# A decode kernel: four-column-tile PV, looped batches, long runs of w3 and w4, and extra matmuls between the last stages

## The chip, the core and the metric

The kernel runs on one core of one Trainium2 chip. The metric is device time in microseconds (us) of one execution; lower is better. Before the change it takes 193.37 us (median of 4 executions).

Each product is a pair of instructions: a weight load (the stationary operand, "PEld" in the profile) and a matmul (which streams the moving operand, "PE"); the page counts 2,028 of each. DVE, ACT and POOL are the vector, scalar and general engines. SP issues the large DMA transfers.

## The reference, cut to what matters

```python
# A: attention of one new token per sequence; B = 8, D = 512, 32 query heads, 8 KV heads, window 2048
q = (layernorm(x) @ wq)                  # wq [512, 4096]
p = softmax(q k^T / sqrt(128))           # k, v: the last 2048 rows of each cache, 8 x 8 x 2048 x 128
h = x + concat_heads(p v) @ wo           # wo [4096, 512]
# B: mixer and MLP. With sequence length 1 the token shift gives zeros: x1 = layernorm(h)
xb = layernorm(h)
h2 = gelu(layernorm(xb) @ w3) @ w4       # w3 [512, 1792], w4 [1792, 512]
out = h + xb + h2
```

K and V are 67 MB, wq and wo 8.4 MB, w3 and w4 3.7 MB: 79.18 MB in all, read once. Everything else is small.

## The kernel before

Per batch, TensorE transposes K (128 small transposes), multiplies by q, and later by V. The last stages, with h kept transposed: `hT` has the 512 features on 4 x 128 partitions.

```python
# loads at the end of the queue: wo (4 parts), w3 (2 halves), w4 (3 parts)
B_w3.rearrange("(k p) f -> p k f", k=KC)[:, k0:k1, :]        # runs of 3,584 B
B_w4.rearrange("(c p j) n -> p c (j n)", p=128, j=2)         # runs of 2,048 B
...
def pe_PV(...):    # per (batch, head group): 16 matmuls of 512 columns, two column tiles of 64
    ins = e.matmul(pv_ps[gq][64*a:64*(a+1), :]..., pT_sb[:, gq, cc, :], vq[:, cc, :, :], ...)
...
def pe_proj(e):    # 32 x 4 pairs: weights are columns of wo, next to each other (step 1)
    for h in range(NJ):
        for k in range(KC):
            ins = e.matmul(hT_ps[:, k*B:(k+1)*B], wo_at(h)[:, k*128:(k+1)*128], opl[:, h, :], ...)
...                # DVE and ACT: statistics, norms, uT
def pe_h3(e):      # 56 pairs: weights are every second column of w3 (step 2)
    w3_sb[:, kc, c*256:(c+1)*256].rearrange("p (q j) -> p j q", j=2)[:, j, :]
...                # gelu on ACT
def pe_fin(e):     # 14 x 4 matmuls of 128 columns, waits for each part of w4
```

The step of h3's weights follows from w4's layout: if a partition holds j consecutive rows of w4, the gelu output must have its rows in that order, so h3 has to pick every j-th column of w3. In the same way, w3's layout fixes the order of `hT`'s features, and with it the step of the columns of wo in the projection.

## Time and profile before

| | before |
|---|---|
| time, us (4 executions) | 193.37 (193.22 to 193.54) |
| DMA | 79.18 MB, engines 99-100% busy from the second slice to the last but one |
| last part of w4 releases its matmuls at | 188.68 us of a span of 191.5 |
| projection / h3 on TensorE | 3.57 / 1.66 us |

From the page of the profile: busy time and share of the span of each engine, and three rows over 40 equal slices (granted TensorE clock in tenths, DMA busy in tenths, GB/s).

```profile
PE 145.9 (76%) x2028; PEld 99.3 (52%) x2028; DVE 105.2 (55%) x287; ACT 90.3 (47%) x113; POOL 1.9 (1%) x14
PEclk9999999999699999999999999999999999999555
DMA  6999999999999999999999999999999999999991
GB/s 221 438 431 428 428 421 431 433 431 424 431 428 428 435 431 438 431 428 431 426 428 438 431 435 430 428 431 428 428 438 431 431 431 431 431 431 401 418 398 54
```

The DMA row says what bounds the kernel: no slice below 9 until the data are through. The last three clock digits are 5: TensorE runs the last stages at half clock.

The chain of work that ended last, in order of time (start us, us, what):

```profile
166.46 21.54 DMA slots<-in_B_w_dram
188.00 0.04 issue
188.04 0.60 PE b L887 x16
188.64 0.03 issue
188.68 0.41 PE b L887 x8
```

It goes from the w4 load straight into the last matmuls. And the timeline of TensorE's tail (start us, us, line, operands, count, idle time before and its releaser):

```profile
178.06 3.57 PE L796 MATMUL S_ps<-opl,slots 128*128 128x8 bf16 x128
184.34 1.66 PE L857 MATMUL misc<-uT,slots 128*128 128x8 bf16 x56 [1.52 <-DVE uT L833]
186.82 1.02 PE L887 MATMUL b<-slots,gT 128*8 128x128 bf16 x32 [0.51 <-DMA slots<-in_B_w_dram]
188.04 1.02 PE L887 MATMUL b<-slots,gT 128*8 128x128 bf16 x24 [0.20 <-DMA slots<-in_B_w_dram]
```

L796 is the projection, L857 is h3, L887 the last stage. The last stage waited for DMA twice, but only 0.51 and 0.20 us: TensorE arrives shortly before its data.

### The profile page before, as it was taken

The page shows a single profiled execution, that of the slowest core. Times are in us where ns is not written, and L with a number is a line of the kernel's source. Part 1 is how long each engine was busy: PE and PEld are TensorE (multiplying, and loading weights), DVE is VectorE, ACT ScalarE, POOL GpSimd, SP SyncE. Part 2 cuts the span into 40 slices and gives each one's busy share as a digit, 9 for nine tenths or more (in the row PEclk, how much of TensorE's full clock was granted, in tenths as well). Part 3 has the DMA queues.
Part 4 walks back from the last instruction along what each step waited for, and adds up shares of the span by engine and source line. Part 5 has one row for each costly group of instructions (what it writes and reads, how often), then busy time and mean ns, then how long its engine had stood idle before and what let it go on. Part 6 is the DMA issues. An engine that isn't in the chain of part 4 may idle for free. (4 is left out here: it accounts for less than half of the span.)

```text
span 191.5 us, 4850 instructions
## 1 busy us (share of the span) xinstructions
PE 145.9 (76%) x2028; PEld 99.3 (52%) x2028; DVE 105.2 (55%) x287; ACT 90.3 (47%) x113; POOL 1.9 (1%) x14
## 2 busy tenths in 40 slices
PE   2027998796899869886989688968896888776854
PEld 0003876582857455645564547553655465343842
DVE  6401757464268474747474747565665657585141
ACT  3301676862656265536643564447344835406041
POOL 4000000000000000000000000000000000000000
PEclk9999999999699999999999999999999999999555
DMA  6999999999999999999999999999999999999991
GB/s 221 438 431 428 428 421 431 433 431 424 431 428 428 435 431 438 431 428 431 426 428 438 431 435 430 428 431 428 428 438 431 431 431 431 431 431 401 418 398 54
DMA packets 6857, 79.31 MB, mean 414 GB/s; under 512 B 688, under 2 KB 704, under 8 KB 2368
## 3 DMA queue, kind: packets, MB, share of 16 engines
q1 hardware_dynamic: 6832, 79.18, 97.5%
q8 instruction: 6, 0.10, 0.2%
q14 instruction: 3, 0.02, 0.0%
q10 hardware_dynamic: 16, 0.01, 0.0%
HBM read 79.18 MB, written 0.01 MB: 414 GB/s over the span
## 5 line engine op out<-in xcount | busy, mean ns | idle before, releaser
L496 ACT ACTIVATE kT_sb<-kT_ps 128x1024 bf16<-128x1024 bf16 x64 | 64.6, 1028 | 67.3 <-PE kT_ps L473 66.9
L473 PE MATMUL kT_ps<-perm_b,slots 128*128 128x128 bf16 x1024 | 68.5, 223 | 22.9 <-PEq L454 22.8
L473 PEld LDWEIGHTS kT_ps<-perm_b,slots 128*128 128x128 bf16 x1024 | 60.8, 100 | 33.7 <-issue 33.7
L500 DVE COPY kT_sb<-kT_ps 128x1024 bf16<-128x1024 bf16 x64 | 43.3, 688 | 27.1 <-PE kT_ps L473 27.1
L516 PE MATMUL S_ps<-kT_sb,qcur 128*32 128x512 bf16 x256 | 22.5, 387 | 0.8 <-PEq L454 0.8
L546 ACT ACTIVATE P_sb<-S_ps,mtile 128x1024 bf16<-128x1024 f32 x16 | 17.8, 1115 | 2.6 <-DVE mtile L537 2.5
L595 PE MATMUL b<-slots,pT_sb 128*64 128x512 bf16 x128 | 16.5, 384 | 1.2 <-PEq L454 1.2
L577 DVE TENSOR_TENSOR pT_sb<-kT_ps,maskT 128x1024 bf16<-128x1024 bf16 x16 | 10.5, 685 | 10.7 <-PE kT_ps L489 10.7
L595 PE MATMUL misc<-slots,pT_sb 128*64 128x512 bf16 x128 | 15.3, 382 | 0.6 <-PEq L454 0.6
L526 DVE TENSOR_REDUCE mtile<-S_ps 128x1 f32<-128x512 f32 x8 | 5.5, 692 | 13.6 <-PE S_ps L516 13.6
L595 PEld LDWEIGHTS misc<-slots,pT_sb 128*64 128x64 bf16 x128 | 6.8, 109 | 8.4 <-issue 3.6
L595 PEld LDWEIGHTS b<-slots,pT_sb 128*64 128x64 bf16 x128 | 6.2, 109 | 9.2 <-issue 5.7
L516 PEld LDWEIGHTS S_ps<-kT_sb,qcur 128*32 128x32 bf16 x256 | 5.3, 93 | 8.3 <-issue 4.2
L489 PEld LDWEIGHTS kT_ps<-ident_b,P_sb 128*128 128x128 bf16 x128 | 7.2, 98 | 4.1 <-issue 4.1
L489 PE MATMUL kT_ps<-ident_b,P_sb 128*128 128x128 bf16 x128 | 8.7, 219 | 0.6 <-PEq L454 0.6
L611 DVE SCALAR_TENSOR_TENSOR o_sum<-b,mrl,o_sum 128x128 f32<-128x128 f32 x24 | 8.4, 351 | 0.8
L611 DVE SCALAR_TENSOR_TENSOR o_sum<-misc,mrl,o_sum 128x128 f32<-128x128 f32 x24 | 8.4, 351 | 0.8
L395 PE MATMUL S_ps<-slots,xlnT 128*8 128x512 bf16 x32 | 3.6, 626 | 5.7 <-DMA slots<-in_A_wq_dram 5.7
L412 DVE TENSOR_SCALAR q_sb<-S_ps 128x512 bf16<-128x512 f32 x1 | 0.7, 692 | 9.1 <-PE S_ps L395 9.1
L626 DVE CAST o_all<-misc 16x128 bf16<-16x128 f32 x7 | 2.0, 279 | 6.4 <-PE misc L620 6.3
L395 PEld LDWEIGHTS S_ps<-slots,xlnT 128*8 128x8 bf16 x32 | 1.0, 117 | 7.4 <-issue 7.4
L657 ACT ACTIVATE opl<-kT_ps 128x224 bf16<-128x224 f32 x1 | 1.2, 1182 | 6.6 <-PE kT_ps L649 6.6
(104 smaller groups left out, 82.5 us busy)
## 6 DMA issues: line engine op xcount, KB each, us to landing
slots<-in_A_k_cache_dram SPq DMA_DIRECT2D x16, 2048.0 KB, 14.2
slots<-in_A_v_cache_dram SPq DMA_DIRECT2D x16, 2048.0 KB, 16.5
slots<-in_A_wq_dram SPq DMA_DIRECT2D x1, 4096.0 KB, 12.3
slots<-in_A_wo_dram SPq DMA_DIRECT2D x1, 2048.0 KB, 30.7
slots<-in_B_w_dram SPq DMA_DIRECT2D x2, 896.0 KB, 32.0
slots<-in_A_wo_dram SPq DMA_DIRECT2D x1, 1024.0 KB, 32.5
slots<-in_A_wo_dram SPq DMA_DIRECT2D x2, 512.0 KB, 33.7
slots<-in_B_w_dram SPq DMA_DIRECT2D x1, 1024.0 KB, 25.7
```

The lines of the kernel that those rows point to most:

```text
L395: ins = e.matmul(S_ps[32 * j:32 * j + B, k, :], xlnT[:, kc * B:(kc + 1) * B], wq_v[:, kc, n0:n0 + 512], start=(kc == 0), stop=(kc == KC - ...
L473: ins = e.matmul(kT_ps[t % 2][:, c * 128:(c + 1) * 128], src[:, c * 128:(c + 1) * 128], perm_b[:, :], is_transpose=True)
L489: ins = e.matmul(kT_ps[half][:, c * 128:(c + 1) * 128], P_sb[:, half * W // 2 + c * 128:half * W // 2 + (c + 1) * 128], ident_b[:, :], is_ ...
L496: e.activation(kT_sb[:, i % NKT, 0:W // 2], kT_ps[i % 2][:, 0:W // 2], ACT.Copy).then_inc(sem_Elo, 1)
L500: e.tensor_copy(kT_sb[:, i % NKT, W // 2:W], kT_ps[i % 2][:, W // 2:W]).then_inc(sem_Ehi, 1)
L516: ins = e.matmul(S_ps[32 * gl:32 * (gl + 1), 0, :], qcur[:, GL * gq + gl, o:o + 32], kv[:, gl, :, :], start=(t == 0), stop=(t == 2 * NT - ...
L526: ins = e.tensor_reduce(mtile[:, 2, 0:1], S_ps[:, 0, :], AX.X, ALU.max)
L546: e.activation(P_sb[:, half * W // 2:(half + 1) * W // 2].rearrange("r (k g) -> r k g", g=GL), s_rep, ACT.Exp, bias=mtile[:, j, 0:1], scal ...
L577: e.tensor_tensor(pT_sb[:, :, half * hc:(half + 1) * hc, :].rearrange("p a c (g x) -> p (c g) a x", g=GL), kT_ps[half][:, 0:W // 2].rearra ...
L595: ins = e.matmul(pv_ps[gq][64 * a:64 * (a + 1), :].rearrange("p (q d) -> p q d", d=DH), pT_sb[:, gq, cc, :], vq[:, cc, :, :], start=(cc < ...
L611: ins = e.scalar_tensor_tensor(o_sum[:, gq, :], pv_ps[gq][:, q * DH:(q + 1) * DH], w[:, q:q + 1], o_sum[:, gq, :], ALU.mult, ALU.add)
L626: e.tensor_copy(o_all[:, gq, b, :], pv_ps[gq][0:GL * R, OT]).then_inc(sem_oT, 1)
```

## The change

Its intent: PV in four column tiles instead of two (64 matmuls of 128 columns per head group in place of 16 of 512), one loop over the batches, a part of wo loaded early, longer DMA runs for w3 and w4, and extra matmuls on spare data so that TensorE's clock does not fall between the last stages. The core of the diff, cut:

```diff
-        def pe_PV(...):  # 16 matmuls of 512 columns per head group, tiles (0, 64a)
+        def pe_PV(e, slot, gq, cs=range(CT)):
+            for c in cs:
+                for q in range(NT):
+                    ins = e.matmul(pv_ps[32 * q:32 * (q + 1), :], pT_sb[:, c, q, 16 * gq:16 * gq + 32],
+                                   slots[:, slot, k * DH:(k + 1) * DH], ..., tile_position=(0, 32 * q))
...  # K has two slots; the four-step weighted sum and the placement stage go; all batches in one loop
+        order = [("k", 0), ("k", 1), ("vl", 0), ("wo", 0)]        # first quarter of wo early
+        for b in range(NB - 1):
+            order += [("k", 2 * b + 2), ("k", 2 * b + 3), ("v", 2 * b), ("v", 2 * b + 1)]
+        order += [("vl", 1), ("wo", 1), ("wo", 2), ("w3", 0), ("w4", 0)]
...
-  B_w3.rearrange("(k p) f -> p k f", k=KC)
+  B_w3.rearrange("(p k) f -> p k f", k=KC)                        # runs of 7,168 B
-  B_w4.rearrange("(c p j) n -> p c (j n)", p=128, j=2)
+  B_w4.rearrange("(p c) n -> p (c n)", c=FC)                      # runs of 8, 4 and 2 KB
...
+        def pe_keep(e, n):
+            for _ in range(n):
+                e.matmul(keep_ps, ident_b[:, 0:32], kT_sb[:, 0, 0:512], start=True, stop=True)
...  # projection: one ahead, one at each of h = 4, 8, 12, 16, 20, 24; weights with step 4
-                    wo_at(h)[:, k * 128:(k + 1) * 128]
+                    wo_at(h).rearrange("r (p k) -> r k p", k=KC)[:, k, :]
...  # statistics: 1 before, 7 after; h3: 1 between the halves, weights with step 14; last stage: 1
-                    w3_sb[:, kc, c * 256:(c + 1) * 256].rearrange("p (q j) -> p j q", j=2)[:, j, :]
+                    w3_sb[:, kc, :].rearrange("r (p c) -> r c p", c=FC)[:, fc, :]
```

That makes 17 extra matmuls.

## The prediction

> **What bounds it now.** The DMA queue. The page's slices show the 16 DMA engines busy 99-100% from the second slice to the last but one, at 421-438 GB/s; queue 1 takes 97.5% of the span for 79.18 MB. In the chain that ended last, the w3/w4 loads are 11% of the span. TensorE (76%), DVE (55%) and ACT (47%) have room. The timeline shows the last w4 piece releasing eight matmuls at 188.68 us; the other 2.8 us are those (0.41 us), two evictions (0.58) and the output DMA. By packet size: 16 KB rows 611 ns (429 GB/s), 8 KB 309 ns, 4 KB 159 ns (412), w3's 3,584 B 140 ns (410), w4's 2,048 B 84 ns (390).
>
> **What changes, costed.**
> 1. PV: 256 matmuls of 512 columns in two column tiles (1.92 us per 16) become 1,024 of 128 columns in four: by columns, half the time. But a pair of weight load and matmul took 27.9 ns in the wo projection; [...] I estimate 64 x 27 ns = 1.7-1.8 us per head group: little saved. DVE loses the four-step weighted sum (1.45 us per group) and the placement stage.
> 2. Looping. My sum for one batch, from trace durations (8 transposes of 1.05, QK 8 x 0.4, P 2 x 0.6, PV 3.6, the rest 1), is 17.5-18.5 us of TensorE against 19.5 us for a batch's 8.4 MB. K has only two slots, but each K tile is asked for 10 us or more before its turn, V about 9. The one thin place: the fourth K tile, asked for near 31 us, due near 33.6. So the queue should stay full, and TensorE wait for K 1-2 us per batch.
> 3. wo's first quarter early: same bytes. The tail chain (last PV near 174.5, wo's last piece 179.6, uT 183, h3 done 184.7) runs ahead of w4 by 1-2 us; before, by only about 0.3.
> 4. Long runs: w3 4.51 us -> estimate 4.30 (7,168 B); w4 4.71 -> 4.42 (8, 4, 2 KB); wo's cuts -0.1. Together about 0.6 us of queue time, all on the critical path.
> 5. Extra matmuls: the granted clock was 0.50 from 178 us on. Warm, proj (3.57 us) and h3 (1.66) shorten, but DMA hides that. On the path only the last eight matmuls: 0.1-0.2 us.
>
> Bytes (79.18 MB) and start are unchanged, so about 0.8 us is all that can be had; the other savings of TensorE and DVE are off the path.
>
> **Predicted: 192.7 us, 80% range 191.8 to 193.8.** Faster by over 2%: 0.03; within 2%: 0.92; slower by over 2%: 0.05.
>
> **What would show it.** DMA slices still 99-100%, the last ones above 401/418/398 GB/s; last w4 landing 0.5-0.7 us earlier; PE waiting for K in each batch; PV at 1.7-1.9 us per 64; granted clock near 1.0 in the tail; the chain still ending in w4; DVE busy down 15-20 us, without effect.
>
> **What would make it wrong.** PV pairs over 43 ns, or loop branches and instruction fetch, taking a batch past 19.5 us: then TensorE bounds, and the loss is eight-fold. The queue running dry near 33 us or at V's reuse: DMA slices below 9 there. The tail chain not ahead of w4: the last matmuls then wait on gelu.

## The result, and the profile after

| | before | after |
|---|---|---|
| time, us (4 executions each) | 193.37 (193.22 to 193.54) | 200.36 (200.03 to 200.71) |
| span of the profiled execution, us | 191.5 | 198.3 |
| projection, first to last matmul, us | 178.06 to 181.6 | 176.31 to 185.2 |
| h3, us | 1.66 | 3.86 with the extra matmul in it |
| last matmul ends, us | 189.1 | 195.9 |

The ratio is 1.0362, with a 95% interval of 1.0336 to 1.0387: slower by 3.6%. Here and below a ratio is the mean time of one kernel's fast runs over that of the other's in the same rounds, so it is not quite the ratio of the medians.

The page, same rows as before:

```profile
PE 151.8 (77%) x2889; PEld 120.0 (61%) x2889; DVE 85.9 (43%) x183; ACT 93.2 (47%) x119; POOL 6.4 (3%) x17
PEclk9999998599979999999699969999998799996585
DMA  6999999999999999999999999999999999999700
GB/s 226 469 397 433 423 423 430 436 433 430 426 421 433 436 436 425 436 423 430 433 443 426 430 430 423 433 436 440 426 433 423 433 430 443 426 409 421 292 0 5
```

DMA is as busy as it was, and is through two slices before the end. The attention part is not slower (the projection starts at 176.31 us instead of 178.06); the 6.8 us are behind it. DVE lost 19 us of work, which does not show in the time.

The chain that ended last, its second half (the pieces left out are more of the same alternation in the projection):

```profile
177.32 1.10 issue
178.42 0.69 PE S_ps L675 x16
179.12 0.32 PE kT_ps L658
179.44 0.63 PE S_ps L675 x16
180.06 0.54 PE kT_ps L658
...
184.07 1.16 PE S_ps L675 x32
185.23 0.54 PE kT_ps L658
185.77 0.67 PE S_ps L694 x2
186.43 3.10 PE kT_ps L658 x7
189.53 1.77 PE misc L739 x28
191.31 0.32 PE kT_ps L658
191.62 1.77 PE misc L739 x28
193.40 0.53 PE b L760 x32
193.93 0.85 PE b L772 x32
```

From 178.42 us on there is only TensorE: no DMA, no wait. L675 is the projection, L658 the extra matmuls, L694 the statistics, L739 h3, L760 the residual, L772 the last stage. Two things stand out. The extra matmuls are on the chain, each 0.32 us at full clock and up to 0.54 at half, and the seven after the statistics take 3.10 us, although uT was ready 1.6 us before they ended (the timeline has uT written from 187.70 to 187.89 us, h3 from 189.47). And 28 pairs of h3 take 1.77 us, 63 ns each, where before 56 pairs took 1.66, 30 ns each.

Did the extra matmuls keep the clock up? The view by windows shows it (window, its length, busy us and count of PE, PEld, DVE, ACT, POOL, then granted clock, DMA share, GB/s):

```profile
179.00:180.00 1.00, 1.00 (x22) 0.74 (x19) 0.00 (x0) 0.00 (x0) 0.00 (x0) 0.83 0.96 404
180.00:181.00 1.00, 1.00 (x17) 0.57 (x16) 0.00 (x0) 0.00 (x0) 0.00 (x0) 0.50 1.04 437
188.00:189.00 1.00, 1.00 (x4) 0.30 (x2) 0.77 (x5) 0.99 (x2) 0.00 (x0) 0.50 0.01 2
190.00:191.00 1.00, 1.00 (x20) 1.00 (x20) 0.00 (x0) 0.00 (x0) 0.00 (x0) 1.00 0.00 0
194.00:195.00 1.00, 1.00 (x44) 0.82 (x34) 0.00 (x0) 0.00 (x0) 0.00 (x0) 0.50 0.00 0
```

No: it fell to 0.50 near 180 us, with PE busy 100% of the time by the profile, and came back only after the seven extra matmuls in a row. In the last stage it was at 0.50 again. DMA is idle from 188 us.

### The profile page after: what moved, and what is told of

Read it like the earlier page. It is cut to its first block, busy times and chain, and to the rows that moved or that the text cites. A ratio compares the mean times of both kernels' runs of the same rounds, so it can differ in the third digit from the quotient of the medians.

```text
span 198.3 us, 6430 instructions
## 1 busy us (share of the span) xinstructions
PE 151.8 (77%) x2889; PEld 120.0 (61%) x2889; DVE 85.9 (43%) x183; ACT 93.2 (47%) x119; POOL 6.4 (3%) x17
## 5 line engine op out<-in xcount | busy, mean ns | idle before, releaser
L476 PE MATMUL S_ps<-kT_sb,qcur 128*32 128x512 bf16 x256 | 22.6, 387 | 2.9 <-PEq L419 2.9
L533 PE MATMUL misc<-slots,pT_sb 128*32 128x128 bf16 x1024 | 16.2, 219 | 1.9 <-PEq L419 1.9
L533 PEld LDWEIGHTS misc<-slots,pT_sb 128*32 128x32 bf16 x1024 | 14.7, 97 | 3.4 <-issue 3.3
L523 DVE TENSOR_TENSOR pT_sb<-kT_ps,mask 128x1024 bf16<-128x1024 bf16 x18 | 12.4, 689 | 3.6 <-PE kT_ps L452 3.5
L452 PE MATMUL kT_ps<-perm_p,P_sb 128*128 128x128 bf16 x144 | 10.9, 218 | 3.0 <-PEq L419 3.0
L452 PEld LDWEIGHTS kT_ps<-perm_p,P_sb 128*128 128x128 bf16 x144 | 8.4, 97 | 5.1 <-issue 4.5
L552 PE MATMUL b<-o_sum,selw 128*128 128x32 f32 x56 | 7.3, 275 | 4.3 <-PEq L419 4.3
L552 PEld LDWEIGHTS b<-o_sum,selw 128*128 128x128 f32 x56 | 6.8, 191 | 5.3 <-issue 5.3
L658 PE MATMUL kT_ps<-kT_sb,ident_b 128*32 128x512 bf16 x17 | 8.4, 567 | 0.0
L675 PEld LDWEIGHTS S_ps<-opl,slots 128*128 128x128 bf16 x128 | 4.8, 118 | 3.6 <-issue 3.4
L284 DVE TENSOR_SCALAR ident_f<-iota_f 128x128 f32<-128x128 f32 x1 | 5.7, 5683 | 1.3 <-POOL iota_f L207 1.3
L675 PE MATMUL S_ps<-opl,slots 128*128 128x8 bf16 x128 | 5.4, 175 | 1.1 <-issue 1.1
L285 DVE TENSOR_SCALAR ident_b<-iota_f 128x128 bf16<-128x128 f32 x1 | 5.6, 5607 | 0.0
```

What stands on the lines that cost most here:

```text
L284: e.tensor_single_scalar(ident_f[:], iota_f[:], 0.0, ALU.is_equal)
L452: ins = e.matmul(kT_ps[half][:, c * 128:(c + 1) * 128], P_sb[:, k * 128:(k + 1) * 128], perm_p[:, :], is_transpose=True)
L476: ins = e.matmul(S_ps[32 * gl:32 * (gl + 1), 0, :], qcur[:, GL * gq + gl, o:o + 32], kv[:, gl, :, :], start=(t == 0), stop=(t == 2 * NT - ...
L523: e.tensor_tensor(bass.AP(tensor=pT_sb[:, :, :, :].tensor, offset=h0 * NT * 48, ap=[[CT * NT * 48, 128], [48, CT // 2 * NT], [32, 2], [1, ...
L533: ins = e.matmul(pv_ps[32 * q:32 * (q + 1), :], pT_sb[:, c, q, 16 * gq:16 * gq + 32], slots[:, slot, k * DH:(k + 1) * DH], start=(gq == 0 ...
L552: ins = e.matmul(op_ps(b), selw[:, q, :], o_sum[:, NJ * q:NJ * (q + 1)], start=(q == 0), stop=(q == 3))
```

## The experiments

Theory S: strided weight reads slow the projection and h3. Theory K: the extra matmuls cost their own queue time. Rivals: the rewrite of attention delays the tail (A); the extra matmuls are needed and failed only in part, or pay where the weights are not strided (C). All twelve kernels gave correct results.

| run | what it is | median us (range) | ratio to before (95%) |
|---|---|---|---|
| a_nokeep | after, no extra matmuls | 195.56 (194.97 to 196.01) | 1.011 (1.008 to 1.014) |
| b_contig | after, short runs, steps 1 and 2 | 196.59 (196.34 to 197.88) | 1.019 (1.015 to 1.023) |
| c_both | both undone | 193.73 (193.21 to 194.79) | 1.0035 (0.9996 to 1.0074) |
| d_before_long | before, long runs alone | 194.99 (194.98 to 195.23) | 1.009 (1.007 to 1.011) |
| e_before_keep | before, extra matmuls alone | 197.91 (197.85 to 199.24) | 1.026 (1.023 to 1.030) |
| f_w3long | after, no extra matmuls, w4 short | 193.78 (193.47 to 195.08) | 1.005 (1.001 to 1.009) |
| g_w4long | after, no extra matmuls, w3 short | 194.48 (194.13 to 194.72) | 1.007 (1.005 to 1.008) |
| h_w4j7 | as g, w4 in runs of 7 rows | 194.44 (193.66 to 195.28) | 1.005 (1.001 to 1.009) |
| i_warm | c_both, extra matmuls at the start | 193.27 (193.21 to 193.49) | 1.0001 (0.9986 to 1.0016) |
| j_w3long_warm | f_w3long, the same start | 193.55 (193.23 to 194.45) | 1.002 (0.999 to 1.004) |
| k_keep64 | b_contig, extra matmuls of 64 columns | 194.22 (193.62 to 194.84) | 1.004 (1.003 to 1.006) |
| l_fit | i_warm, 4 extra matmuls in the tail's waits | 193.40 (193.18 to 194.04) | 1.0002 (0.9987 to 1.0017) |

### Undo one half, the other half, both: a_nokeep, b_contig, c_both

```diff
# a_nokeep
-            for _ in range(n):
+            for _ in range(0):
                 e.matmul(keep_ps, ident_b[:, 0:32], kT_sb[:, 0, 0:512], start=True, stop=True)
# b_contig: w3, w4, the projection's and h3's weights as in the kernel before (and the small residual matmuls that depend on w3's order)
-  B_w3.rearrange("(p k) f -> p k f", k=KC)        -> "(k p) f -> p k f"
-  B_w4.rearrange("(p c) n -> p (c n)", c=FC)      -> "(c p j) n -> p c (j n)", j=2
# c_both: the two together
```

> The kernel after with none of the 17 extra matmuls. Theory K (their queue time costs): the chain from the second wo stage on holds five extra matmuls of 0.3-0.54 us in the projection, 1.6 us by which h3 starts after uT is ready, 0.3 between h3's halves: about 4.5 us less, so 195.5-196.3 us, still slower than before (193.4), because h3 still takes 63 ns a pair. Rival C (the extra matmuls are needed to keep the clock up and only failed in part): without them the tail gets slower, 201 us or more. Rival A (the attention rewrite delays the tail): no change, 200.4.

> The kernel after, with w3 and w4 loaded in the short runs of before, so that the weights of the projection are read with step 1 and those of h3 with step 2 (instead of 4 and 14); extra matmuls kept. Theory S (strided weight reads cost): projection 39 -> 28 ns a pair, h3 63 -> 29 ns a pair, 1.2 + 1.9 = about 3.1 us less: 197.0-197.6 us. If the step does not matter and the 63 ns come from the clock or from the extra matmuls: 200 us or more, since the DMA gets 0.2-0.5 us slower.

> Both undone; the rest of the change (four-column-tile PV, loop, early wo) stays. Theories S and K together: TensorE's chain ends before w4 has landed (near 188.9 us), so the time is that of before, 193.0-193.8 us, bounded by DMA again, and the gains of the two single runs do not add up to more than 7 us. Rival A (attention rewrite costs): stays at 195 us or above.

The three fell as theories S and K had it, b_contig a little below its range. Without the extra matmuls 4.8 us are gone, without the strides 3.8, without both 6.6 (differences of medians; the executions of each of these three runs spread by 1.0 to 1.6 us). The two single gains add up to 8.6; what is missing in c_both is that DMA bounds again. Its chain, to be compared with that of before:

```profile
159.59 28.47 DMA slots<-in_B_w_dram
188.06 0.04 issue
188.10 0.60 PE b L773 x8
188.70 0.04 issue
188.74 0.41 PE b L773 x8
```

So rival A falls: with the new PV, the loop and the early part of wo in place, the end is where it was (188.74 against 188.68 us). The 0.4 us that the median still lacks come from two of its four executions (194.79 and 194.14 us): the scatter treated below. Rival C falls for the kernel after. Now h3 in the timelines. In a_nokeep (step 14):

```profile
185.87 3.53 PE L739 MATMUL misc<-uT,slots 128*128 128x8 bf16 x56 [1.52 <-DVE uT L714]
```

In b_contig (step 2, one extra matmul between the halves):

```profile
188.61 0.90 PE L741 MATMUL misc<-uT,slots 128*128 128x8 bf16 x28
189.76 0.86 PE L741 MATMUL misc<-uT,slots 128*128 128x8 bf16 x28
```

And in c_both (step 2):

```profile
184.19 1.66 PE L741 MATMUL misc<-uT,slots 128*128 128x8 bf16 x56 [1.52 <-DVE uT L715]
```

Step 14 takes 3.53 us without any extra matmul, step 2 takes 1.66. And the clock does not matter to this stage: a_nokeep ran its 56 pairs at a granted clock of 0.50, the kernel after ran its second 28 in 1.77 us at 1.00, which is the same 63 ns. With step 2, c_both ran at 0.50. A window of h3 in a_nokeep and one in c_both, columns as above:

```profile
187.00:188.00 1.00, 1.00 (x20) 1.00 (x19) 0.00 (x0) 0.05 (x1) 0.00 (x0) 0.50 0.49 191
184.00:185.00 1.00, 0.81 (x30) 0.81 (x31) 0.86 (x6) 1.00 (x1) 0.00 (x0) 0.50 1.04 403
```

b_contig ran it mostly at 1.00; the windows of its h3:

```profile
189.00:190.00 1.00, 1.00 (x31) 0.75 (x28) 0.00 (x0) 0.00 (x0) 0.00 (x0) 0.91 0.00 0
190.00:191.00 1.00, 0.86 (x37) 0.66 (x37) 0.00 (x0) 0.26 (x1) 0.00 (x0) 1.00 0.00 0
```

That is 30 ns a pair at 0.50 and, from the chain of b_contig (0.83 and 0.80 us per 28), 29 ns at 1.00. There was nothing to win here by a warm clock. Only the last stage, with 128 columns to stream, gains: its first 32 matmuls take 0.62 us in b_contig (clock 1.00) and 1.02 in c_both (0.50), and 1.03 in the kernel after, where the clock had fallen again to 0.50.

That it is the weight load that the stride slows can be read from the loads of h3 themselves (shortest, median and longest, ns). First a_nokeep (step 14), then c_both (step 2):

```profile
L739 PEld LDWEIGHTS misc<-uT,slots x56: 138/160/162, 185.9 to 189.1; 128*128 128x128 bf16 x56
L741 PEld LDWEIGHTS misc<-uT,slots x56: 103/104/118, 184.2 to 185.7; 128*128 128x128 bf16 x56
```

### Each half alone on the kernel before: d_before_long, e_before_keep

```diff
# d_before_long: before, with the loads and weight steps of w3 and w4 from after
+  B_w3.rearrange("(p k) f -> p k f", k=KC)        # projection weights with step 4
+  B_w4.rearrange("(p c) n -> p (c n)", c=FC)      # h3 weights with step 14
# e_before_keep: before, with pe_keep at the same places, on its own spare PSUM tile
+  keep_ps = kT_ps[1][:, :].bitcast(dt.float32)[0:32, 0:512]
```

> The kernel before with only the long runs of w3 and w4 and the strided weight reads that follow from them. Theory S: the projection goes from 3.57 to about 5.0 us, h3 from 1.66 to 3.5, minus the 0.3 us of slack before w4: 196.0-196.6 us. If the long runs are good as such: 192.8-193.2 us.

> The kernel before with only the 17 extra matmuls added at the same places (on its own spare PSUM tile). Theory K: six of them sit in the projection at 0.3-0.54 us, the seven after the statistics take 3.1 us where the DVE needs 2.2 for uT; TensorE's chain ends 3.5-5 us later: 197.0-198.4 us. Rival C (a warm clock repays them where the weights are read with step 1 or 2): 193.5 or less.

d_before_long lost 1.65 us, not the 3 that I expected: the projection took 4.43 us, 35 ns a pair instead of the 39 that I had read off stretches of 16 pairs with extra matmuls between, and the last stage, now later than its data, no longer waits. h3 took 3.52 us as expected. The two stages grew by 2.7 us together and cost 1.65: the tail before had about 1.1 us of slack, not the 0.3 that I had read. In e_before_keep the cost of the extra matmuls shows without any stride: 197.91 us, 4.7 over the kernel before, as theory K has it. Its projection never ran at more than 0.50: with one extra matmul after every 16 pairs the clock did not rise here either.

### Which stride: f_w3long, g_w4long, h_w4j7

```diff
# f_w3long: a_nokeep, but w4 in runs of 2 rows: projection step 4, h3 step 2
# g_w4long: a_nokeep, but w3 as before: projection step 1, h3 step 14
# h_w4j7: g_w4long, but
-  B_w4.rearrange("(p c) n -> p (c n)", c=FC)
+  B_w4.rearrange("(c p j) n -> p c (j n)", p=128, j=7)    # runs of 7, 5 and 2 KB, h3 step 7
```

> The kernel after without extra matmuls, w3 in long runs (projection weights with step 4), w4 in the short runs of before (h3 weights with step 2). Theory S: the projection keeps its 35-39 ns a pair, h3 falls from 63 to about 29 ns: TensorE is just ahead of w4 again, 193.1-194.5 us. If it is w3's layout that hurts: 195 or above.

> The kernel after without extra matmuls, w4 in long runs (h3 weights with step 14), w3 in the short runs of before (projection weights with step 1). Theory S: projection 28 ns, h3 63 ns a pair: h3 ends 1.9 us later than with step 2, of which some 1.2 us are slack: 193.9-195.2 us.

> As the run before, but w4 in runs of seven rows, so that h3's weights have step 7. Theory S, if the cost grows with the step: 40-50 ns a pair, h3 2.3-2.8 us, which fits ahead of w4: 193.0-194.3 us. If any step above 2 costs the same, h3 takes 63 ns a pair as with 14.

f and g fell in their ranges; h lies 0.1 us above. The timelines give the cost by step: 110 pairs of the projection in 3.10 us (c_both, step 1) and in 3.83 us (f_w3long, step 4), 56 pairs of h3 in 1.66, 3.15 and 3.54 us (steps 2, 7, 14).

| step of the weights' columns | 1 | 2 | 4 | 7 | 14 |
|---|---|---|---|---|---|
| ns a pair, 128 weight columns, 8 moving columns | 28 | 30 | 35 | 56 | 63 |

Steps 1 and 4 are from the projection, the others from h3. For step 4, d_before_long shows the same rate at both clocks: the view by windows counts 35 matmuls, with those that reach across an edge, in the us from 179 to 180 (clock 1.00) and 35 in that from 181 to 182 (0.50). So step 7 costs nearly as much as 14, more than my 40 to 50, and step 4 little. It is w4's layout that hurts; w3's cost fits into the slack. What the long runs of w4 win, 0.3 us of queue time by packet durations, is far less than the 1.9 us that they cost in h3.

### The scatter, and extra matmuls that fit: i_warm, j_w3long_warm, k_keep64, l_fit

The new attention part leaves one thing: c_both scatters from 193.2 to 194.8 us, while before stays within 193.2 to 193.7. In some profiles the eighth slice of the GB/s row dips. This is the row of a_nokeep's page:

```profile
GB/s 225 433 426 429 429 421 441 362 426 433 433 431 429 433 426 428 433 433 433 433 433 429 433 433 433 433 429 433 433 426 433 429 433 433 433 433 401 426 288 8
```

And the same row of c_both's page:

```profile
GB/s 221 438 438 424 421 424 428 435 431 438 435 423 421 438 431 429 431 435 435 424 431 431 435 428 435 431 435 438 421 428 435 428 435 431 438 435 405 407 398 42
```

The SP's timeline has the issue of the third and fourth K tile, merged (start, length of the two). In a_nokeep:

```profile
24.21 7.98 SPq L246 DMA_DIRECT2D slots<-in_A_k_cache_dram  x2
```

And in c_both:

```profile
22.29 8.00 SPq L246 DMA_DIRECT2D slots<-in_A_k_cache_dram  x2
```

Where the third K tile was issued at 22.0-22.6 us and the fourth eight later, there is no dip (after, c, f, g, i, j); where at 23.6-24.2, the slice has 360-375 GB/s (a, b, h, k, l). An estimate from the row: 70 GB/s less in a slice of 4.8 us is 0.8 us lost. What makes it late is TensorE at the start: in a_nokeep the first 64 transposes take 5.55 us, in the kernel after twice 1.95 us for 32. The granted clock fits this, though the window view prints 1.00 throughout: it does so wherever the trace has no clock record yet. In the packed traces the first record, at full clock, lies at 21.1 to 22.2 us in the five profiles with the dip and at 12.6 to 16.7 us in the six without. In l_fit, with the dip, the window view counts 12, 12 and 13 matmuls in the three us from 18 to 21 and 19 in the next; later, where c_both has clock records, it counts 12 to 13 in a us at 0.50 (37 to 40 us) and 19 at 1.00 (41 to 42).

```diff
# i_warm: c_both, and ahead of the query projection, where TensorE waits for wq
+            for _ in range(4):   # and 3 more after the transposes of the normed x
+                e.matmul(kT_ps[0]...[0:32, 0:512], ident_b[:, 0:32], <ident_b, repeated to 512 columns>)
# j_w3long_warm: f_w3long with the same start
# k_keep64: b_contig with
-                e.matmul(keep_ps, ident_b[:, 0:32], kT_sb[:, 0, 0:512], ...)
+                e.matmul(keep_ps[:, 0:64], ident_b[:, 0:32], kT_sb[:, 0, 0:64], ...)
# l_fit: i_warm, and pe_keep(3) after the statistics, pe_keep(1) before the wait for the gelu; no others
```

> The run with both undone (193.2 to 194.8 us, where before scatters by 0.3), plus seven extra matmuls where TensorE is idle anyway, just ahead of the query projection. Theory W (the scatter comes from the clock at the start: where the first transposes run at half clock, the load of the fourth K tile is issued near 31.7 us instead of 29.6 and the DMA queue runs thin near 34-38 us): the fourth K load issued by 30.2 us in the profile, no dip in the GB/s row, all executions within 193.1-193.6. If the scatter has another cause: still executions at 194-195.

> The same start, w3 in long runs (projection weights with step 4), w4 short, no extra matmuls in the tail. DMA-bound by then: w4 lands 0.1-0.2 us earlier, but TensorE's chain is just as late: 193.0-193.5 us, no scatter.

> The run with step 1 and 2 and all 17 extra matmuls (196.6 us), but each with 64 columns instead of 512. Theory K (it is their queue time that costs, not their presence or the switching): about 0.05-0.1 us each at half clock, so 193.2-194.8 us, as with none. If their mere presence costs (switching, ordering): 196 us or more.

> Both undone, the warm start, and only four extra matmuls of 512 columns, placed where TensorE waits for longer than they take: three after the statistics (1.3 us at half clock in a gap of 1.5) and one ahead of the wait for the gelu. Theory K: they cost nothing, 193.0-193.5 us. If they also bring the clock up for the last stage, its last eight matmuls take 0.2 us less: 192.9-193.2.

i_warm came out as expected: 193.27 us, all five executions within 0.3. But that the extra matmuls at the start are the cure is not shown: with the same start, j missed its range and reached 194.45 once, in the profiled execution of l_fit the transposes still took 5.14 us and the queue dipped, and four kernels without that start (after, c, f, g) had quick transposes too. So the link from late transposes to the dip held in eleven of eleven profiles of this family; what makes the clock rise early in some executions is open.

k_keep64 shows that it is the length of the extra matmuls that costs: the same 17, with 64 columns, cost 0.5 us over c_both's median instead of 2.9 (c_both was measured in other rounds); and its profiled execution had the dip. l_fit shows the same from the other side: three of full length in a gap of 1.5 us cost nothing (h3 took 1.66 us right behind them). They did not raise the clock either; the last seven matmuls of its chain take 0.41 us, as before.

No version beats the kernel before; the best, i_warm, equals it. In c_both, i_warm and l_fit the chain that ended last goes through the w4 load again; in the other nine runs it goes through TensorE's own tail.

## Why the prediction was wrong, point by point

- **What bounds the kernel before: right**, and in the kernel after DMA is just as busy until its data are through, at 188 us. But I put too much weight on it: a bound that holds with about 1 us of slack is two bounds.
- **Point 5 is the step that failed first**: "proj (3.57 us) and h3 (1.66) shorten, but DMA hides that". The extra matmuls were taken as free and as effective. They sit in the same queue, in order, and on the chain they took 2.5 us in the projection, 1.6 us beyond uT and 0.3 in h3. The clock fell in spite of them, so most cost 0.54 us instead of 0.32; and even a full clock would not have shortened these stages (63 ns a pair at 0.50 and 1.00 with step 14; 30 and 29 with step 2; 35 matmuls counted in a us at both with step 4). Undoing them gave 4.8 us.
- **Point 3 failed with it**: "The tail chain ... runs ahead of w4 by 1-2 us". I costed the tail with durations from before. The weights' access pattern is in the diff, and I read it as an index, not as a cost: step 4 took 35 ns a pair and step 14 took 63, against 28 and 30. Undoing the strides gave 3.8 us. I had uT at 183 us and h3 done at 184.7; they came at 187.9 and 193.4. With both, the chain's last matmul ends at 195.9 us instead of 189.1: the overlap with w4 that the forecast rests on was gone.
- **Point 4: the size was right, its worth was not.** By packet size w3 took 4.38 us and w4 4.41 (2.47 + 1.27 + 0.67), 0.43 less than before, where I had estimated 0.5. The queue was off the path by then.
- **Point 1 was mis-sized**: 128 pairs in column tiles took 1.97 us, so 64 take 1.0 us and not 1.7-1.8; the halving by columns came in full. The 27 ns a pair, my estimate for the column tiles, did not hold: they took 15. DVE fell by 19 us, as said. Neither shows in the time.
- **Point 2 was right**: DMA full, and TensorE standing still for 1.70 us between one batch's last matmul and the next batch's transposes (in the timeline near 55 us). The thin place at the fourth K tile was real, and costs some executions about 0.8 us.
- **What would make it wrong** named the right place ("The tail chain not ahead of w4") and gave it too little chance: 5% for slower, when I had read the slack before as only 0.3 us. The reason it named, a wait for gelu, is not what the kernel after shows: there the last matmuls wait for TensorE itself.

One piece stays open. In the whole family of after, TensorE stands still for 1.1 to 2.0 us early in the projection with no releaser in the profile ("177.32 1.10 issue" above). A packet of 16 KB on the queue for instructions ends about when the gap begins (177.22 us in after), so it may be a wait for instructions; no run tested it. In the kernel after its 1.10 us are on the chain. In c_both DMA hides it, but it takes most of the lead that point 3 counted on: the projection starts 1.8 us earlier than before (176.27 us), stands still for 1.50, and ends only 0.15 earlier.

## What to carry to other kernels

Where two chains end within about a microsecond of each other, cost both after the change, not just the one that ends last now; and cost every access pattern that a new DMA layout forces on the engines that read it (here step 14 took 63 ns a pair, step 2 took 30). An extra matmul to keep the clock up takes its place in the queue at the clock that is granted, not the one hoped for (here up to 0.54 us at 0.50 against 0.32 at 1.00): put it only where TensorE waits longer than it takes, and first check that the stage behind it depends on the clock at all (h3 did not: 63 ns a pair at both). Undo the parts one by one and together: here two losses of 4.8 and 3.8 us overlapped, and what remained was the old bound.

## What these runs measured of the hardware

- Pairs with 128 weight columns and 8 moving columns took 28, 30, 35, 56 and 63 ns at steps 1, 2, 4, 7 and 14, the same at clocks of 0.50 and 1.00 where a run shows both (within 1 ns at steps 2 and 14, by the window counts at step 4).
- In four column tiles, 128 pairs of 128 columns took 1.97 us, 15 ns a pair. My prediction rested on an estimate of 27 ns a pair.
- In the kernel after, the clock fell to 0.50 near 179.7 us, 1.2 us after a gap of 1.1 us had ended, and stayed there through more than 6 us in which the profile shows PE busy without a break: one matmul of 512 columns after every 16 pairs of 8 columns did not hold or raise it. It rose 0.4 to 1.2 us after the end of seven in a row, in all three kernels that had seven of 512 columns (after, b_contig, e_before_keep), and in the kernel after it fell again 3.4 us later. That the seven raised it is the likely reading, but no run varied their number alone.
- By median packet duration, in the kernel after, rows of 2 KB moved at 390 GB/s over 16 engines, 4 KB at 412, 7 KB at 422, 16 KB at 429.
